# Casts of the folded w2 on GpSimd, later outputs, later reuse of slots, and a sync queue in emission order, in a fused attention and SwiGLU kernel

## The chip, the cores and the metric

The kernel runs on one core of one Trainium2 chip. The metric is the time of one execution on the device in microseconds (us). The engines are named as in the profile: PE is TensorE's matmuls, PEld its weight loads, DVE is VectorE, ACT is ScalarE, POOL is GpSimd, and SP is SyncE, whose queue issues nearly all of the transfers (DMAs).

## What is computed

The input x has 2048 tokens of 512 elements in fp32. Cut to what matters, the reference is:

```python
xn  = layernorm(x)
qkv = (xn @ wqkv)                      # 32 heads of 16
a   = softmax(mask(q @ k.T / sqrt(16))) @ v   # sliding window of 256 tokens
A   = a @ wo
B   = (silu(xn @ w1) * (xn @ w3)) @ w2   # 512 -> 1792 -> 512
out = x + A * silu(B)                  # the kernel's last step
```

The last line is written as the kernel joins the two halves: one output block takes the product with wo, the silu of the feed-forward result and x.

## The kernel before, in words

**Work.** Every matmul of the projections and of the feed-forward part is done on operands that are split in two fp16 pieces, a high and a low one, in three products (high by high, high by low, low by high). The tokens are taken in four tiles t of 512. A tile's attention is 8 units (32 units in all), each a group of heads over the sliding window. A tile's feed-forward part is 14 blocks f of 128 hidden columns: `gate_up` (matmuls at L991, tanh on ACT at L1006, two products on DVE at L1010 and L1015) and then the product with w2, called down. In t=0 down is `down` at L1184, with w2 split as it comes. In t=1 to 3 it is a fast matrix product with seven products in place of eight: activations are folded on POOL and ACT (`fold_first`, L1042 to L1054, and `fold_second`, to L1084, with casts at L1072, subtractions at L1073 and sums at L1078 to L1081), and the 14 blocks are taken in two groups k, of 8 and of 6. A group's seven pieces are `fold_down_piece` (L1114); `unfold` (L1148) puts the seven results together.

**Weights.** In t=0 w1, w3 (L836) and w2 (L877) are loaded raw and split on ACT and POOL (helper lines L329 to L334); the split w1 and w3 are stored to DRAM as dW1 (L997), the split wqkv as dWQ (L589). From t=1 on they come back from there (dW1 at L832, dWQ at L617). The folded w2 is made once, in `fold_weights` (L934 to L976), for seven pairs j of blocks, about when tile 1 begins: raw w2 is loaded (L943) and scaled on ACT (L949), the sums z and y are made on POOL (L951 to L954), and `cut` makes of each of e, o (the scaled rows themselves), z and y a high piece with a cast on ACT (L959) and a low piece with subtractions on POOL (L961). Four steps later the result is stored to dW2 (L966). `load_fold` (L1095) fetches from dW2 the weights of each piece, two pieces ahead of the piece that uses them: 84 loads in three tiles.

**Attention's small transfers.** A unit's maxima go out and come back through DRAM (dm at L691, back into qa at L693). Queries and keys are fetched at L626. The finished results go os to on (L780, four transfers) and their denominators os to dd (L781), dd to dr (L795), after a reciprocal on DVE (L799, L800) dr to de (L802), de to rb (L806, eight transfers); then POOL multiplies by rb (L807 through the helper L329) and casts (L813).

**Output.** `total` (L1209 to L1241) makes one block of 128 tokens: tanh on ACT (L1222), the product with wo on PE (L1228), a product on DVE (L1232), the addition of x on POOL (through L329; on DVE in the last tile), and the store (L1237). Its x comes by `residual` (L1207).

**What sets the order.** Feed-forward pieces are put between the pieces of attention by `spread` and `batches`. A counter of steps, `step`, runs what `later(n, f)` put off by n steps. Working tiles come from a pool of 55 slots: `take` hands out the slot that has been free longest, and `give(tile, after=n)` returns a slot with a date n steps on, so that it is handed out later. `ORDERED` (L54) names the engines whose instructions are issued in the order in which the program emits them. In the kernel before that is PE alone: the queues of ACT, DVE, POOL and SP are put in an order of its own by a scheduler, and `tc.issue_after` holds an instruction behind another one in that order. An engine's queue, once compiled, is strictly in order: an instruction that waits holds all that stand behind it.

Of the kernel before, what the change touches and what calls it, by code (L numbers as in the profile page):

```python
# [17 lines left out]
ENGINE = mybir.EngineType  # L18
# [3 lines left out]
P = 128  # L22
S = 2048
D = 512
# [22 lines left out]
KR = TERMS * DH  # L47
# [3 lines left out]
VW = DH + 1  # L51
VB = 10
SLOTS = 55
ORDERED = {ENGINE.PE}  # L54
GROUPS = ((0, 4), (4, 8), (8, 11), (11, 14))
FOLDS = ((0, 4), (4, 7))
FOLD_AT = (0, 1, 2, 4, 6, 8, 10)
# [25 lines left out]
def tile_block(ctx: ExitStack, tc: tile.TileContext, x, wqkv, wo, w1, w3, w2, out):  # L83
# [142 lines left out]
    dW1 = dram.tile([FB, 2, P, 2 * NC * P], F16, name="dW1")  # L226
    dW2 = dram.tile([7, P, FB // 2, D], F16, name="dW2")


    def squares(parts, on_act=0, apart=0):  # L230

# [335 lines left out]
    def project(t, g, k, terms=(range(3),), scores_bank=False):  # L567


        cell = {}  # L570

        parts = ([[(c, i) for c in (2 * half, 2 * half + 1) for i in range(3)] for half in range(2)] if len(terms) == 1
                 else [[(c, i) for i in group for c in range(NC)] for group in terms])

        def part(n):
            assert turned[t] == 4
            w = WQ[t, g, k]
            xh, xl = X[t]
            if n == 0:
                cell["pp"] = pss.tile([P, 2, TW], F32, name="s")[:, 0, :] if scores_bank else bank([P, TW])  # L580
            for c, i in parts[n]:
                a, b = ((0, xh), (1, xh), (0, xl))[i]
                nc.tensor.matmul(cell["pp"], w[:, (a * NC + c) * P:(a * NC + c + 1) * P], b[:, c, :], start=(c, i) == parts[0][0],  # L583
                                 stop=(c, i) == parts[-1][-1])
            if n < len(parts) - 1:
                return
            if t == 0:
                def store():
                    nc.sync.dma_start(dWQ[g, k], w)  # L589
                    give(w, after=4)  # L590
                later(8, store)
            else:
                give(w)
            pp = cell["pp"]
            both = take(F16)
            B = both.rearrange("p (a t) -> p a t", a=2)
            s = QS / (XS * WS)
            with urgent():
                nc.scalar.activation(B[:, 0, :], pp, AF.Copy, scale=s)

            def rest():
                with urgent():
                    lasts["emptied"] = nc.vector.scalar_tensor_tensor(B[:, 1, :], pp, s, B[:, 0, :], op0=ALU.mult, op1=ALU.subtract)  # L603
                d = (dQ, dK)[k][g][:, :, t * TW:(t + 1) * TW]
                if k == 0:
                    nc.sync.dma_start(d[:, 0:2, :], B[:, 0:1, :].to_broadcast([P, 2, TW]))
                    nc.sync.dma_start(d[:, 2, :], B[:, 1, :])
                else:
                    nc.sync.dma_start(d[:, 0:2, :], B)
                    nc.sync.dma_start(d[:, 2, :], B[:, 0, :])  # L610
                give(both, after=4)
            later(1, rest)
        return opening([(len(l), lambda n=n: part(n)) for n, l in enumerate(parts)])
# [5 lines left out]
    def fetch(t, g):  # L619
        QA[t, g] = qa = qpool.tile([P, 4, TW], F16, name="qa")  # L620
        ka = keys(t, g)
        c0 = 0 if t else 2 * P
        for dst, d in ((ka[:, :, c0:], dK[g][:, :, t * TW - 2 * P + c0:(t + 1) * TW]),
                       (qa, dQ[g][:, :, t * TW:(t + 1) * TW])):
            for r in range(2):
                nc.sync.dma_start(dst[64 * r:64 * r + KR],  # L626
                                  d[64 * r:64 * r + 64].rearrange("(a d) i t -> (d i) a t", d=DH))


# [197 lines left out]
    def load(t, f):  # L827
        if t:
            a = [take(F16) for _ in range(2)]
            WF[t, f] = [a, None]  # L830
            for k in range(2):
                nc.sync.dma_start(a[k], dW1[f, k])  # L832
            return
        RAW[f] = raw = [take(F32) for _ in range(2)]
        for k, w in enumerate((w1, w3)):
            nc.sync.dma_start(raw[k].rearrange("p (c f) -> p c f", f=P),  # L836
                              w[:, f * P:(f + 1) * P].rearrange("(c p) f -> p c f", p=P))

    measured = set()
# [34 lines left out]

    def load_down(f):
        RAW2[f] = raw = take(F32)
        nc.sync.dma_start(raw, w2[f * P:(f + 1) * P, :])  # L877

    def measure_down(k, f):

# [53 lines left out]
    def fold_weights(j):  # L934

        cell = {}
        l, r = slice(0, 256), slice(256, 512)
        sub = nc.gpsimd.tensor_sub

        def load():  # L940
            cell["raw"] = [take(F32) for _ in range(2)]
            for i, raw in enumerate(cell["raw"]):
                nc.sync.dma_start(raw, w2[(2 * j + i) * P:(2 * j + i + 1) * P, :])  # L943

        def sums():
            assert folded
            e, o = cell["raw"]
            for i, raw in enumerate((e, o)):
                nc.scalar.activation(raw, raw, AF.Copy, scale=fold_w[:, 2 * j + i:2 * j + i + 1])  # L949
            cell["z"] = z, y = [take(F32) for _ in range(2)]  # L950
            sub(z[:, l], e[:, r], e[:, l])  # L951
            sub(z[:, r], o[:, r], z[:, l])
            sub(y[:, l], o[:, r], e[:, r])
            sub(y[:, r], o[:, l], z[:, r])  # L954

        def cut(raw, n, which):

            a = take(F16)
            nc.scalar.copy(a[:, 0:n], raw[:, 0:n])  # L959
            for c in range(0, n, 256):  # L960
                sub(a[:, n + c:n + c + 256], raw[:, c:c + 256], a[:, c:c + 256])  # L961
            give(raw, after=6)

            def store():
                for c, i in enumerate(which):
                    nc.sync.dma_start(dW2[i, :, j, :].rearrange("p (h d) -> p h d", h=2),  # L966
                                      a[:, 0:2 * n].rearrange("p (h c d) -> p c h d", h=2, d=256)[:, c])
                give(a, after=4)
            later(4, store)

        def cuts():
            e, o = cell["raw"]
            z, y = cell["z"]
            for n, work in enumerate(((e, 256, (0,)), (o, 512, (1, 2)), (z, 512, (4, 5)), (y, 512, (6, 3)))):
                later(2 * n, lambda work=work: cut(*work))
        return load, sums, cuts  # L976
# [3 lines left out]
    def gate_up(t, f):  # L980
        cell = {}

        def part(k, half):
# [10 lines left out]
                return  # L994
            if t == 0:
                def store():
                    nc.sync.dma_start(dW1[f, k], w)  # L997
                    give(w, after=4)
                later(8, store)
            else:  # L1000
                give(w)
            if k == 0:
                cell["s"] = sg = take(F32)

                with urgent():
                    nc.scalar.activation(sg, cell[0], AF.Tanh, scale=sg_scale[:, f:f + 1])  # L1006

                def product():
                    with urgent():
                        lasts["emptied"] = nc.vector.scalar_tensor_tensor(sg, sg, 1.0, cell[0], op0=ALU.add, op1=ALU.mult)  # L1010
                later(1, product)
            else:
                sg = cell["s"]
                with urgent():
                    lasts["emptied"] = nc.vector.scalar_tensor_tensor(sg, cell[1], 0.5 * HS / (WS * XS)**2, sg,  # L1015
                                                                      op0=ALU.mult, op1=ALU.mult)
                if t:
                    HH[t, f] = sg
                    later(1, lambda: (fold_second if f % 2 else fold_first)(t, f // 2))
                    return  # L1020
                HH[t, f] = hh = take(F16)

                def rest():
                    nc.scalar.copy(hh[:, 0:TW], sg)  # L1024
                    halves(nc.gpsimd.tensor_sub, hh[:, TW:], sg, hh[:, 0:TW])
                    give(sg, after=4)
                later(1, rest)
        return [q for k in range(2) for q in opening([(6, lambda k=k, half=half: part(k, half)) for half in range(2)])]

# [27 lines left out]
    def fold_second(t, j):  # L1057
# [7 lines left out]
        def cut(raw, view, which, give_too=()):  # L1065
# [7 lines left out]
                sub(lo[:, k], view[:, k], hi[:, k])  # L1073
            for k, i in enumerate(which):
                operand(t, j, i, made, 512, 256 * k)
            give(raw, *give_too, after=4)

        nc.gpsimd.tensor_add(z[:, 0], ee[:, 1], oo[:, 1])  # L1078
        sub(z[:, 1], z[:, 0], ee[:, 0])
# [8 lines left out]
    def load_fold(t, k, i):  # L1088
# [3 lines left out]
        for j in range(j0, j1, 2):  # L1092
            made.append(take(F16))
            n = min(2, j1 - j)
            nc.sync.dma_start(made[-1].rearrange("p (j d) -> p j d", d=D)[:, 0:n], dW2[i, :, j:j + n, :])  # L1095

    QS7 = {}

# [39 lines left out]
    def unfold(t):  # L1138
# [14 lines left out]
        into(0, 0, q[0], q[1])  # L1153
        halves(add, q[5], q[5], q[4])
        into(0, 1, q[5], q[2])
        give(*q, after=6)
        summed.update((t, b) for b in range(4))

    def folds(t, k):
# [353 lines left out]
    for n in range(len(units)):  # L1513
# [6 lines left out]
                    ahead[n].append((0, lambda k=k, half=half: load_qk(*tiles[k], half)))  # L1520
        if n % 8 >= 4 and t < NT - 1:
            beside[n] += value(4 * t + n % 8)
        if 2 <= n % 8 < 6 and t:
            beside[n] += [(0, lambda t=t, b=n % 8 - 2: residual(t - 1, b))] + total(t - 1, n % 8 - 2)
        beside[n] += ahead[n]
    other = [sum(c for c, _ in b) for b in beside]
    a_unit = (whole - KEEP - EARLY + sum(other)) / len(units)
# [55 lines left out]
```

## Time and profile before

| | |
|---|---|
| time of the kernel before | 861.5 us, median of 3 runs (861.15 to 862.03) |
| time of the profiled execution | 859.68 us |
| its span, first to last instruction | 857.9 us |
| mean granted clock of PE | 0.982 |
| PE busy | 804.5 us of the span |
| DVE, POOL, ACT busy | 635.0, 416.1, 402.1 us |
| bytes moved by DMA | 133.82 MB, mean 156 GB/s |

A row of a group of instructions reads: line, engine, operation, output and input tiles, shape, number; then the busy time in us and the mean of one in ns; then how long the engine had been idle ahead of them and what ended most of that. A row of a timeline reads: start, duration, engine and line, and in brackets the idle time ahead of it with its releaser. For SP ("SPq") the duration is the issue of the transfers, not their landing. The window view gives the busy time of each engine in a stretch, and PEclk, the granted clock.

### The profile page before, as it was taken

The page shows a single profiled execution, that of the slowest core. Times are in us where ns is not written, and L with a number is a line of the kernel's source. Part 1 is how long each engine was busy: PE and PEld are TensorE (multiplying, and loading weights), DVE is VectorE, ACT ScalarE, POOL GpSimd, SP SyncE. Part 2 cuts the span into 40 slices and gives each one's busy share as a digit, 9 for nine tenths or more (in the row PEclk, how much of TensorE's full clock was granted, in tenths as well). Part 3 has the DMA queues.
Part 4 walks back from the last instruction along what each step waited for, and adds up shares of the span by engine and source line. Part 5 has one row for each costly group of instructions (what it writes and reads, how often), then busy time and mean ns, then how long its engine had stood idle before and what let it go on. Part 6 is the DMA issues. An engine that isn't in the chain of part 4 may idle for free.

```text
span 857.9 us, 24287 instructions
## 1 busy us (share of the span) xinstructions
PE 804.5 (94%) x9302; PEld 420.7 (49%) x9302; DVE 635.0 (74%) x2027; ACT 402.1 (47%) x597; POOL 416.1 (49%) x723
## 2 busy tenths in 40 slices
PE   8998988999999499998999898999999989999997
PEld 4444444444444245654447454456544644457464
DVE  8886796788886378675888777875688778774447
ACT  6899774544565244453443233443444334334411
POOL 2248064341768936346362746421146458551561
PEclk9999999999999799999999999999999999999999
DMA  9999654248356483757554444554545545324411
GB/s 283 259 286 293 197 156 124 90 131 238 90 166 177 113 232 111 231 173 218 163 155 122 152 115 137 144 157 125 160 121 144 138 141 152 109 83 129 127 34 62
DMA packets 118421, 133.82 MB, mean 156 GB/s; under 512 B 19168, under 2 KB 76832, under 8 KB 118304
## 3 DMA queue, kind: packets, MB, share of 16 engines
q1 hardware_dynamic: 118016, 131.74, 52.4%
q8 instruction: 73, 1.20, 0.6%
q10 hardware_dynamic: 288, 0.52, 0.2%
q14 instruction: 44, 0.36, 0.2%
HBM read 94.50 MB, written 33.42 MB: 149 GB/s over the span
## 4 chain that ended last, share of the span: by engine, by line
PE 56%; DVE 14%; POOL 11%; DMA 6%; ACT 5%; issue 4%; SPq 2%; POOLq 0%; ACTq 0%; DVEq 0%
PE m L991 21%; PE m L1114 10%; PE po L758 6%; PE m L583 5%; DVE junk L664 4%; PE m L1228 4%; PE s L730 4%; DMA slot<-in_B_w_dram 3%; POOL slot L329 3%; PE m L553 2%; POOL slot L1073 2%; PE s L650 2%; PE m L1184 2%; DVE s L737 2%; ACT pt L740 1%
## 5 line engine op out<-in xcount | busy, mean ns | idle before, releaser
L991 PE MATMUL m<-XH,slot 128*128 128x512 f16 x896 | 272.9, 387 | 7.5 <-DVE slot L603 4.5
L740 ACT ACTIVATE pt<-s,es 128x1024 f32<-128x1024 f32 x152 | 167.6, 1113 | 157.8 <-DVE s L737 154.7
L991 PEld LDWEIGHTS <-slot 128*128 128x128 f16 x1344 | 126.2, 99 | 166.8 <-issue 28.3
L329 POOL TENSOR_TENSOR slot<-slot,slot 128x256 f16<-128x256 f32 (+1 forms) x156 | 104.2, 697 | 146.0 <-ACT slot L1024 68.2
L991 PE MATMUL m<-XL,slot 128*128 128x512 f16 x448 | 172.5, 385 | 0.0
L737 DVE TENSOR_TENSOR s<-s,MK 128x256 f32<-128x256 f32 (+2 forms) x280 | 119.2, 435 | 57.6 <-PE s L730 54.4
L664 DVE CUSTOM_DVE_ANT_0 junk<-s,MW 128x320 bf16<-128x320 f32 x276 | 134.1, 486 | 20.5 <-PE s L650 11.6
L1114 PE MATMUL m<-slot,slot 128*128 128x256 f16 x882 | 102.7, 273 | 1.9 <-POOL slot L1073 1.2
L1114 PEld LDWEIGHTS <-slot 128*128 128x128 f16 x882 | 84.4, 98 | 19.1 <-issue 5.1
L664 DVE CUSTOM_DVE_ANT_0 junk<-po,MW 128x320 bf16<-128x320 f32 x172 | 83.6, 486 | 5.7 <-DVE al L288 0.5
L583 PE MATMUL m<-XH,slot 128*128 128x512 f16 x240 | 72.4, 386 | 12.8 <-DVE slot L1010 12.8
L1073 POOL TENSOR_TENSOR slot<-slot,slot 128x256 f16<-128x256 f32 x126 | 82.7, 676 | 0.6
L758 PE MATMUL po<-pt,V 64*32 64x320 f32 (+4 forms) x2880 | 77.2, 342 | 0.0
L1010 DVE SCALAR_TENSOR_TENSOR slot<-slot,m 128x512 f32<-128x512 f32 x56 | 38.3, 684 | 43.7 <-ACT slot L1006 43.6
L730 PE MATMUL s<-qa,KA 50*64 50x320 f16 (+3 forms) x1472 | 59.2, 261 | 7.2 <-ACT pt L740 5.0
L583 PEld LDWEIGHTS <-slot 128*128 128x128 f16 x384 | 36.1, 99 | 56.7 <-issue 17.4
L758 PEld LDWEIGHTS po<-pt,V 64*32 64x32 f32 x2880 | 50.3, 106 | 22.3 <-issue 0.8
L730 PEld LDWEIGHTS <-KA 50*64 50x64 f16 x1472 | 31.0, 106 | 58.4 <-issue 38.9
L1078 POOL TENSOR_TENSOR slot<-slot,slot 128x256 f32<-128x256 f32 x21 | 15.3, 728 | 89.4 <-DVE slot L1015 89.4
L1006 ACT ACTIVATE slot<-m,sgs 128x512 f32<-128x512 f32 x56 | 38.2, 682 | 37.9 <-PE m L991 37.8
L329 POOL TENSOR_TENSOR on<-on,rb 128x256 f32<-128x256 f32 x32 | 23.4, 752 | 57.4 <-DMA rb<-de 57.3
L650 PE MATMUL s<-KA,qa 48*64 48x320 f16 (+3 forms) x824 | 45.4, 296 | 4.0 <-ACT pt L740 2.4
(186 smaller groups left out, 1170.7 us busy)
## 6 DMA issues: line engine op xcount, KB each, us to landing
slot<-dW SPq DMA_DIRECT2D x147, 256.0 KB
slot<-in_B_w_dram SPq DMA_DIRECT2D x56, 256.0 KB
slot<-in_A_x_dram SPq DMA_DIRECT2D x30, 256.0 KB
dW<-slot SPq DMA_DIRECT2D x28, 256.0 KB
KA<-dK SPq DMA_DIRECT2D x24, 288.0 KB
dW<-slot SPq DMA_DIRECT2D x49, 128.0 KB
qa<-dQ SPq DMA_DIRECT2D x32, 192.0 KB
slot<-dWQ SPq DMA_DIRECT2D x24, 256.0 KB
```

What stands on the lines that cost most here:

```text
L329: op(out[:, c], a[:, c], b[:, c])
L583: nc.tensor.matmul(cell["pp"], w[:, (a * NC + c) * P:(a * NC + c + 1) * P], b[:, c, :], start=(c, i) == parts[0][0], stop=(c, i) == parts[ ...
L650: nc.tensor.matmul(s[c:c + w, r, :n], qa[rows, 2 * p + a, ii * P + c:ii * P + c + w], ka[rows, 2 * p + a, e - n:e], start=True, stop=True)
L664: lasts["maximum"] = nc.vector.tensor_tensor_reduce(out=junk[:, :n], in0=s[:, r, :n], in1=mask, scale=1.0, scalar=NEG, op0=ALU.add, op1=AL ...
L730: nc.tensor.matmul(s[64 * h:64 * h + 64, r, o:o + 64 * n], ka[rows, 2 * p + a, 64 * (m + 4):64 * (m + 5)], qa[rows, 2 * p + a, 64 * (m + k ...
L737: nc.vector.tensor_add(v, v, MK[:, kind, of:of + n, :].unsqueeze(1).to_broadcast([P, 2 * len(which), n, 64]))
L740: nc.scalar.activation(pt, s, AF.Exp, scale=es)
L758: nc.tensor.matmul(cell["po"][32 * i:32 * i + 32, h, 64 * (m + k):64 * (m + k + n)], V[64 * h:64 * h + 64, (4 * t + m // 2) % VB, hd * VW: ...
L991: nc.tensor.matmul(cell[k], w[:, (a * NC + c) * P:(a * NC + c + 1) * P], b[:, c, :], start=c == 0 and i == 0, stop=c == NC - 1 and i == 2)
L1010: lasts["emptied"] = nc.vector.scalar_tensor_tensor(sg, sg, 1.0, cell[0], op0=ALU.add, op1=ALU.mult)
L1073: sub(lo[:, k], view[:, k], hi[:, k])
L1114: nc.tensor.matmul(ps, made[:, f:f + P], wj[:, 256 * b:256 * b + 256], start=j == j0 and n == 0, stop=j == j1 - 1 and n == 2)
```

## The change

- SP joins the engines that issue in emission order. The sync queue takes every transfer where the program emits it.
- `behind_load` holds stores to dWQ (L589, the one shown), dW1 (L997) and dW2 (L966) behind the latest load that the program has recorded in `lasts["load"]` (at L626, shown, and in the same way at L832, L836, L877 and L1095).
- In `fold_weights`, `cut` makes the casts of z and y on GpSimd, each in two halves of 256 columns: 28 casts of 128x256 on POOL in place of 14 of 128x512 on ACT. Those of e and o stay on ACT.
- Slots are returned with later dates: raw of `cut` 14 in place of 6, raw of `fold_second` 14 in place of 4, sg in t=0 8 in place of 4, q of `unfold` 16 in place of 6.
- `total` and `residual` of the tile before come one unit later in the units of t=2 and t=3; in t=1 they stay where they were. The last tile's own are unchanged.

The compiled programs hold the same 944 transfers on SP and the same matmuls.

```diff
-ORDERED = {ENGINE.PE}
+ORDERED = {ENGINE.PE, ENGINE.SP}
...
+    def behind_load():
+        return tc.issue_after(lasts["load"].ins) if "load" in lasts else nullcontext()
...
-                    nc.sync.dma_start(dWQ[g, k], w)
+                    with behind_load():
+                        nc.sync.dma_start(dWQ[g, k], w)
...
-                nc.sync.dma_start(dst[64 * r:64 * r + KR],
+                lasts["load"] = nc.sync.dma_start(dst[64 * r:64 * r + KR],
...
         def cut(raw, n, which):
             a = take(F16)
-            nc.scalar.copy(a[:, 0:n], raw[:, 0:n])
+            if any(raw is r for r in cell["raw"]):
+                nc.scalar.copy(a[:, 0:n], raw[:, 0:n])
             for c in range(0, n, 256):
+                if not any(raw is r for r in cell["raw"]):
+                    nc.gpsimd.tensor_copy(a[:, c:c + 256], raw[:, c:c + 256])
                 sub(a[:, n + c:n + c + 256], raw[:, c:c + 256], a[:, c:c + 256])
-            give(raw, after=6)
+            give(raw, after=14)
...
-                    give(sg, after=4)
+                    give(sg, after=8)
...
-            give(raw, *give_too, after=4)
+            give(raw, *give_too, after=14)
...
-        give(*q, after=6)
+        give(*q, after=16)
...
-        if 2 <= n % 8 < 6 and t:
-            beside[n] += [(0, lambda t=t, b=n % 8 - 2: residual(t - 1, b))] + total(t - 1, n % 8 - 2)
+        b = n % 8 - (2 if t == 1 else 3)
+        if 0 <= b < 4 and t:
+            beside[n] += [(0, lambda t=t, b=b: residual(t - 1, b))] + total(t - 1, b)
```

More of the change, by code (lines that the diff above doesn't have):

```diff
@@ L831, in load @@
             for k in range(2):
-                nc.sync.dma_start(a[k], dW1[f, k])
+                lasts["load"] = nc.sync.dma_start(a[k], dW1[f, k])
             return
@@ L835, in load @@
         for k, w in enumerate((w1, w3)):
-            nc.sync.dma_start(raw[k].rearrange("p (c f) -> p c f", f=P),
+            lasts["load"] = nc.sync.dma_start(raw[k].rearrange("p (c f) -> p c f", f=P),
                               w[:, f * P:(f + 1) * P].rearrange("(c p) f -> p c f", p=P))
@@ L876, in load_down @@
         RAW2[f] = raw = take(F32)
-        nc.sync.dma_start(raw, w2[f * P:(f + 1) * P, :])
+        lasts["load"] = nc.sync.dma_start(raw, w2[f * P:(f + 1) * P, :])
     def measure_down(k, f):
@@ L958, in cut @@
             a = take(F16)
-            nc.scalar.copy(a[:, 0:n], raw[:, 0:n])
+            if any(raw is r for r in cell["raw"]):
+                nc.scalar.copy(a[:, 0:n], raw[:, 0:n])
             for c in range(0, n, 256):
+                if not any(raw is r for r in cell["raw"]):
+                    nc.gpsimd.tensor_copy(a[:, c:c + 256], raw[:, c:c + 256])
                 sub(a[:, n + c:n + c + 256], raw[:, c:c + 256], a[:, c:c + 256])
-            give(raw, after=6)
+            give(raw, after=14)
             def store():
                 for c, i in enumerate(which):
-                    nc.sync.dma_start(dW2[i, :, j, :].rearrange("p (h d) -> p h d", h=2),
-                                      a[:, 0:2 * n].rearrange("p (h c d) -> p c h d", h=2, d=256)[:, c])
+                    with behind_load():
+                        nc.sync.dma_start(dW2[i, :, j, :].rearrange("p (h d) -> p h d", h=2),
+                                          a[:, 0:2 * n].rearrange("p (h c d) -> p c h d", h=2, d=256)[:, c])
                 give(a, after=4)
@@ L996, in store @@
                 def store():
-                    nc.sync.dma_start(dW1[f, k], w)
+                    with behind_load():
+                        nc.sync.dma_start(dW1[f, k], w)
                     give(w, after=4)
@@ L1094, in load_fold @@
             n = min(2, j1 - j)
-            nc.sync.dma_start(made[-1].rearrange("p (j d) -> p j d", d=D)[:, 0:n], dW2[i, :, j:j + n, :])
+            lasts["load"] = nc.sync.dma_start(made[-1].rearrange("p (j d) -> p j d", d=D)[:, 0:n], dW2[i, :, j:j + n, :])
     QS7 = {}
```

## The prediction

> **What bounds the kernel now.** I read the page first, then PE's waits by stretch, then the timelines of ACT and PE around the longest wait, then SP's queue.
>
> ```profile
> span 857.9 us, 24287 instructions
> PE 804.5 (94%) x9302; PEld 420.7 (49%) x9302; DVE 635.0 (74%) x2027; ACT 402.1 (47%) x597; POOL 416.1 (49%) x723
> PEclk9999999999999799999999999999999999999999
> L991 PE MATMUL m<-XH,slot 128*128 128x512 f16 x896 | 272.9, 387 | 7.5 <-DVE slot L603 4.5
> ```
>
> PE is busy for 804.5 of 857.9 us, so at most 53.4 us can be won without touching its work, and the change touches none of it. A gain must come out of PE's pauses. The one slice with a granted clock below 0.9 is the 14th, 279 to 300 us. The waits of PE from 150 to 300 us, and the timelines of ACT and of PE there, show why:
>
> ```profile
> PE m L583 <- DVE slot L1010: 12.2, 2, 11.0
> ```
>
> ```profile
> 287.74 1.45 ACT L959 CAST slot<-slot 128x256 f16<-128x256 f32 x3 [9.01 <-POOL slot L1073]
> ...
> 294.67 0.68 ACT L1006 ACTIVATE slot<-m,sgs 128x512 f32<-128x512 f32 x1
> ```
>
> ```profile
> 296.12 1.01 PE L583 MATMUL m<-XH,slot 128*128 128x512 f16 x2 [11.03 <-DVE slot L1010]
> 296.93 0.63 PE L583 MATMUL m<-XL,slot 128*128 128x512 f16 x1
> ...
> 300.92 0.38 PE L583 MATMUL m<-XL,slot 128*128 128x512 f16 x1
> ```
>
> This is the **knot**. ACT stands for 9.01 us before a cast of `fold_weights`, whose slot POOL (L1073) still holds. The tanh (L1006) is behind it in ACT's queue, DVE's product behind the tanh, PE behind DVE, which stands for 11.03 us. Then PE runs at half clock: 0.63 us for a matmul that takes 0.38 later. From 296.1 to 299.7 us, 3.6 us x (1 - 0.38/0.63) = 1.4 us. The knot costs 12.4 us in all.
>
> **Why POOL is late there.** Windows of 250 to 317, 284 to 300 and 395 to 403 us, and the groups of POOL and of ACT from 205 to 345 us (ACT's with shapes apart):
>
> ```profile
> 250.00:317.00 67.00, 53.75 (x675) 25.43 (x668) 40.24 (x122) 31.81 (x49) 51.71 (x85) 0.90 0.58 170
> 284.00:300.00 16.00, 4.97 (x31) 1.92 (x29) 2.67 (x8) 6.21 (x11) 15.94 (x28) 0.68 0.44 119
> 395.00:403.00 8.00, 5.66 (x43) 2.31 (x42) 3.33 (x11) 5.15 (x7) 5.08 (x8) 0.79 0.48 148
> ```
>
> ```profile
> L961 POOL TENSOR_TENSOR slot<-slot,slot 128x256 f16<-128x256 f32 x35 | 22.7, 677 | 11.5 <-ACT slot L959 11.5
> L1072 POOL CAST slot<-slot 128x256 f16<-128x256 f32 x16 | 6.2, 399 | 4.7 <-issue 4.5
> ```
>
> ```profile
> L959 ACT CAST slot<-slot 128x512 f16<-128x512 f32 x15 | 9.0, 615 | 12.4 <-POOL slot L1073 5.4 <-POOL slot L952 3.1 <-DMA dK<-slot 1.6
> ```
>
> POOL is the fullest engine of that stage after PE (15.94 of 16 us inside the knot), and it stood still for 11.5 us because it waited for ACT's casts: each engine held the other.
>
> **The change part by part.**
>
> *Casts of z and y.* 28 casts of 128x256 on POOL at 0.399 us (L1072, the same shape) add 11.2 us to POOL; 14 casts at 0.615 us take 8.6 us off ACT. POOL's low pieces no longer wait for ACT, and the cast that held the tanh is e's or o's alone. With that and the later reuse of raw (14 steps), the wait of 9.01 us goes: **-12.4 us** with its clock.
>
> What is late next: I laid POOL's queue of the changed program, in its compiled order, out with the durations of these groups from 250.4 us on. It is 113 instructions and 70.6 us without a gap, up to the subtraction L961 that ends at 321. A tanh of the first output block (L1222) waits for that subtraction's slot, and stands in ACT's compiled order ahead of an exp:
>
> ```profile
> 320.18 0.62 ACT L1222 ACTIVATE slot<-slot 128x512 f32<-128x512 f32 x1
> 322.80 1.11 ACT L740 ACTIVATE pt<-s,es 128x1024 f32<-128x1024 f32 x1 [2.00 <-DVE s L737]
> ```
>
> If the knot is gone, that exp is due at 322.8 - 12.4 = 310.4, and the tanh lets it start at about 321.6: 11.2 us late. From both sides: 0, if POOL's work does not delay it; 11.2, if all of it does. I take **+9**, near the upper end, as POOL's queue has no gap in which to catch up; with a half-clock window, **+1.4**. So the knot mostly moves.
>
> *The sync queue in emission order.* In before, SP's order differs: loads stand far ahead. Of `load_fold`'s 84 loads the first and the last issue at 300.0 and 811.1 us; the pieces that use them run later. The instructions of L1095 and then those of L1114 in four windows (336 to 376, 452 to 478, 667 to 692, 765 to 795):
>
> ```profile
> L1095 SPq DMA_DIRECT2D slot<-dW x84: 319/376/1336, 300.0 to 811.1; - x84
> ```
>
> ```profile
> L1114 PE MATMUL m<-slot,slot x168: 272/273/283, 338.1 to 373.9; 128*128 128x256 f16 x168
> ```
>
> ```profile
> L1114 PE MATMUL m<-slot,slot x126: 269/273/283, 453.0 to 475.8; 128*128 128x256 f16 x126
> ```
>
> ```profile
> L1114 PE MATMUL m<-slot,slot x126: 272/273/283, 667.8 to 689.8; 128*128 128x256 f16 x126
> ```
>
> ```profile
> L1114 PE MATMUL m<-slot,slot x168: 272/273/283, 766.5 to 792.8; 128*128 128x256 f16 x168
> ```
>
> In the changed program a load stands where it is emitted, two pieces ahead of its use (2 x 35.8/7 = 10 us in the first of these groups, 2 x 22.8/7 = 6.5 in the second), behind every transfer emitted before it. Those wait for engines, one in line. SP in before, 324 to 374 us and its waits:
>
> ```profile
> 336.55 0.36 SPq L1237 DMA_DIRECT2D out_dram<-slot  x1
> ...
> 350.63 0.38 SPq L691 DMA_DIRECT2D dm<-mt  x1
> ...
> 354.79 0.55 SPq L693 DMA_DIRECT2D qa<-dm  x2
> ...
> 371.79 2.24 SPq L806 DMA_DIRECT2D rb<-de  x5
> ```
>
> ```profile
> SPq L780 <- DVE os L774: 33.8, 10, 7.2
> SPq L693 <- DMA dm<-mt: 21.1, 16, 3.3
> ...
> SPq L1237 <- POOL slot L329: 16.3, 7, 5.9
> ```
>
> An issue costs 2.24/5 = 0.45 us; a transfer through DRAM and back holds the queue for 354.79 - 350.63 = 4.2 us at most. For the landing of a 256 KB load I take 3.4 us (an estimate between nothing and that 4.2, near the upper end since it moves more).
>
> First group of t=1: the output store issues when POOL's addition is done, 336.55, and in emission order 37 transfers stand from it to a load of a piece. 37 x 0.45 = 16.6, and waits of 2.7 (rb for de), 0.8 (L780) and 3.8 (qa for dm) that those transfers meet: issue at 336.6 + 23.9 = 360.5, landed at 363.9. The piece runs at 354.1 in before: 9.8 us late. Bounds 0 and 9.8: the store's own addition moves earlier if the knot shrinks, and one late load gives the rest time. I take the middle, **+5**.
>
> The other groups by the same walk. Second of t=1: L1095 issues at 459.0 and 470.5, lands at 462.4 and 473.9, needed at 460.9 and 469.5: up to 4.4, I take **+3.5**. Second of t=2: issue 679.6, landed 683.0, needed 678.5: 4.5, **+4**. First of t=3, behind the moved output stores: issue 789.0, landed 792.4, needed 788.4: 4.0, **+3**. The first of t=2 has slack.
>
> Second of t=3, the last thing ahead of the end; SP and PE there:
>
> ```profile
> 810.13 1.33 SPq L1095 DMA_DIRECT2D slot<-dW  x3
> ...
> 824.53 2.44 SPq L780 DMA_DIRECT2D on<-os  x4
> 827.02 0.53 SPq L781 DMA_DIRECT2D dd<-os  x1
> 828.72 0.33 SPq L795 DMA_DIRECT2D dr<-dd  x1
> ```
>
> ```profile
> 826.50 3.00 PE L1114 MATMUL m<-slot,slot 128*128 128x256 f16 x26
> 830.72 11.09 PE L1114 MATMUL m<-slot,slot 128*128 128x256 f16 x100 [1.21 <-POOL slot L1073]
> ```
>
> The first loads of this group are emitted directly ahead of it, behind L780, L781, L795 and two loads of x: issue at 828.7 + 0.3 + 2 x 0.45 = 829.9, landed at 833.3, needed at 827.2. 6.1 late, of which 1.2 is spent now in waiting for POOL: 4.9, I take **+4.5**. Each of these groups lies between 0 (the queue is ahead after all) and the figure of the walk.
>
> *Clock.* A pause of 2.34 us brings a half-clock window as well:
>
> ```profile
> 398.10 0.42 PE L730 MATMUL s<-qa,KA 50*64 50x320 f16 x11 [2.34 <-ACT pt L740]
> ```
>
> The window 395 to 403 has 0.79: 8 x 0.21/0.5 = 3.4 us at half clock, 1.4 us lost. Of the five new stalls I charge one in full, **+1.4** (0 to 7). [...]
>
> *The rest at nothing.* In t=0 the raw loads (L836, L877) also lose their lead; the walk leaves them 0 to 13 us of slack, so 0, with -2 to +2. `behind_load` does nothing once SP is in emission order: the last load is already ahead. Later dates only change which slot is taken. Later outputs: the same matmuls, one unit on, PE has the work either way; their stores are priced in the walk.
>
> **Sum.** -12.4 + 9 + 1.4 + 5 + 3.5 + 4 + 3 + 4.5 + 1.4 = +19.4 us. Against the profiled execution 859.7 + 19.4 = 879.1. The median is 1.8 above that execution: 880.9. I predict **881 us**.
>
> **Rivals.**
> *The knot goes and does not form again; loads late:* 861.5 - 12.4 + 21.4 - 4 (the output store comes earlier) = 866.5, say 867. For it: the tanh (L1222) may be given its place where POOL is through. Against: POOL has 70.6 us of work without a gap.
> *The other side, faster:* the queue keeps up, since two pieces give it 6.5 to 10 us; the knot is gone without return. It decides at one point: whether the loads of the pieces issue less than 6.5 - 3.4 = 3.1 us after they are emitted. Then 861.5 - 12.4 + 2 = 851. For it: nothing in before waits long on loads. Against: SP's waits of 33.8, 21.1 and 16.3 us are in line now.
> *Delay feeds on itself:* full 11.2, 9.8 and the walk's figures of the groups (4.4, 4.5, 4.0, 4.9), 7 of clock: 861.5 - 12.4 + 1.4 + 45.8 = 896.
> *It does not do what it says:* the casts change nothing, as the wait is for L1073 and not for z or y, and the queue is hidden: 861.5.
>
> **How the numbers follow.** Forecast 0.57 (its own range 871 to 891), knot gone with late loads 0.18, faster 0.13, worse 0.07, as before 0.05. The range from 862 to 898 leaves out the faster case, the unchanged one and a tail: 0.2. A measurement of this kernel tells 0.2% (1.7 us) from no change. Faster by more: 0.14; within: 0.04; slower: 0.82.
>
> **What would show it.** In the changed profile PE should wait at L1114 for DMAs into slots (dW), several us in t=1 and t=3, where it now waits for none; the wait of 11.0 us at L583 should be gone from 285, and one of like size stand near 310 to 325, behind an exp (L740) or a tanh with ACT waiting for L961. POOL should hold 28 more casts and ACT 14 fewer. If PE shows no wait on those loads, the walk of the queue is wrong; if ACT has no wait of over 4 us on POOL from 300 to 330, the second knot is.

## The result and the profile after

The changed kernel takes 958.5 us (median of 3 runs, 955.3 to 959.35) against 861.5: 1.113 times as long, with an interval of 1.111 to 1.116. The direction was forecast, the size was not: +97 us where +19 were forecast, outside the range.

The lines of the changed file have moved. L583 is now L587, L617 is L622, L650 is L655, L664 is L669, L689 is L694, L691 is L696, L693 is L698, L730 is L735, L740 is L745, L774 is L779, L780 is L785, L802 is L807, L806 is L811, L832 is L837, L959 is L965, L961 is L969, L966 is L975, L991 is L1000, L1006 is L1016, L1010 is L1020, L1073 is L1083, L1095 is L1105, L1114 is L1124, L1222 is L1232, L1237 is L1247, and the helper L329 is L333. First the page of the profile after:

```profile
span 953.5 us, 24246 instructions
PE 824.9 (87%) x9302; PEld 426.1 (45%) x9302; DVE 636.1 (67%) x2027; ACT 395.7 (41%) x583; POOL 426.4 (45%) x751
PEclk9999998998999697999798899989999999999989
L587 PE MATMUL m<-XH,slot 128*128 128x512 f16 x240 | 80.5, 424 | 63.2 <-DMA slot<-dWQ 54.2
```

The span grew by 95.6 us, and two terms make it up. PE is busy 20.4 us longer with the same 9302 matmuls, because more of them ran at half clock (PE is busy for 67.2 us at a granted clock of 0.50 where before had 23.9; the row of the granted clock has six 8s, two 7s and a 6 where before had one 7; the mean is 0.945 against 0.982). The other 75.2 us are pauses: PE stands still for 128.6 us of the span instead of 53.4, with nineteen pauses of over 2 us instead of five. PE's waits in the changed kernel say for what:

```profile
PE m L587 <- DMA slot<-dWQ: 54.2, 8, 13.9
PE m L1124 <- DMA slot<-dW: 18.9, 7, 6.3
PE m L1000 <- DMA slot<-dW: 14.7, 3, 8.0
PE s L735 <- DMA qa<-dm: 11.3, 1, 11.3
PE m L587 <- DVE slot L1020: 8.5, 4, 5.5
```

Read each as: what waited and for what, us in total, times, the longest. Four DMAs hold PE for 99.1 us. In before no DMA held it for more than 0.5. The largest, the loads of the projection weights from dWQ, has no term in the prediction at all. The loads of the folded w2 (L1124), on which the prediction spent its sum, cost 18.9.

Set matmul by matmul against before, in the times of before, the changed kernel is 0.8 us ahead at 220, 8.6 ahead at 310, 13.9 behind at 330, 73 behind at 480 and 95.6 behind at the end. Tile 1 loses most: its stretch has the stores of the folded w2, the backlog of GpSimd and the output stores in one queue.

Two places show the mechanism. The first, in SP's timeline:

```profile
286.93 0.38 SPq L975 DMA_DIRECT2D dW<-slot  x1
302.25 2.45 SPq L785 DMA_DIRECT2D on<-os  x4
...
313.71 0.33 SPq L696 DMA_DIRECT2D dm<-mt  x1
317.66 0.55 SPq L698 DMA_DIRECT2D qa<-dm  x2
```

The queue stands from 287.3 to 302.2 before on<-os. GpSimd's timeline there ends with

```profile
301.54 0.68 POOL L333 TENSOR_TENSOR slot<-on,slot 128x256 f16<-128x256 f32 x1
```

the last read of the tile on by the earlier unit. There is one buffer of on, so the transfer into it must wait for GpSimd's backlog. The maxima were ready long before, as DVE's timeline shows, and are emitted behind on<-os:

```profile
292.73 0.27 DVE L694 CAST mt<-s 32x128 f16<-32x128 f32 x1
```

Their store goes out 20.7 us after 293.0: 9.2 us of that are the rest of the hold, the other 11.5 the sixteen transfers that stand between, with their own waits. PE waits for it:

```profile
319.13 0.85 PE L735 MATMUL s<-qa,KA 50*64 50x256 f16 x8 [11.30 <-DMA qa<-dm]
```

The second place is 50 us later, SP again:

```profile
351.32 0.34 SPq L1247 DMA_DIRECT2D out_dram<-slot  x1
351.70 1.27 SPq L807 DMA_DIRECT2D de<-dr  x1
354.30 3.56 SPq L811 DMA_DIRECT2D rb<-de  x8
...
362.92 2.44 SPq L785 DMA_DIRECT2D on<-os  x4
...
365.98 0.44 SPq L622 DMA_DIRECT2D slot<-dWQ  x1
```

An output store waits for GpSimd's addition, which ends at 351.3; the transfers of the denominators for a round trip through DRAM, 2.6 us from de<-dr to rb<-de; on<-os for GpSimd's use of rb and on, which ends at 362.9; and a weight load that waits for nothing stands last. PE needed it at 354.8:

```profile
368.70 1.03 PE L587 MATMUL m<-XH,slot 128*128 128x512 f16 x2 [13.94 <-DMA slot<-dWQ]
369.52 0.63 PE L587 MATMUL m<-XL,slot 128*128 128x512 f16 x1
```

In before the load for this place was issued at 321.88, for a matmul at 340.70, as these rows of SP and PE of the kernel before show:

```profile
321.88 0.32 SPq L617 DMA_DIRECT2D slot<-dWQ  x1
```

```profile
340.70 0.59 PE L583 MATMUL m<-XH,slot 128*128 128x512 f16 x2
```

The program emits it only 3.1 us ahead of that matmul (at the PE instruction of 337.6 us, by the order of emission in the compiled program). The scheduler had let it issue 15.7 us ahead of that place. Over all 24 such loads, before issues them 7 to 54 us ahead of the place where the program emits them, and eight of them are emitted 3.1 us or less ahead of their use. In the changed kernel they issue between 3 us before and 23 us behind that place. Seven of the eight waits for dWQ, 50.5 of the 54.2 us, stand at loads of these eight.

### The profile page after: what moved, and what is told of

The parts are those of the page before. It is cut to its first block, busy times and chain, and to the rows that moved or that the text cites. A ratio compares the mean times of both kernels' runs of the same rounds, so it can differ in the third digit from the quotient of the medians.

```text
span 953.5 us, 24246 instructions
## 1 busy us (share of the span) xinstructions
PE 824.9 (87%) x9302; PEld 426.1 (45%) x9302; DVE 636.1 (67%) x2027; ACT 395.7 (41%) x583; POOL 426.4 (45%) x751
## 4 chain that ended last, share of the span: by engine, by line
PE 50%; DMA 15%; DVE 10%; POOL 9%; SPq 9%; issue 4%; ACT 3%; DVEq 0%; POOLq 0%; ACTq 0%
PE m L1000 16%; PE m L1124 8%; PE m L587 7%; PE po L763 5%; DMA slot<-dW 3%; PE s L735 3%; DVE junk L669 3%; PE m L1238 3%; PE m L1194 3%; PE m L557 3%; SPq L785 3%; DMA slot<-dWQ 2%; DMA dm<-mt 2%; POOL slot L333 2%; SPq L811 2%
## 5 line engine op out<-in xcount | busy, mean ns | idle before, releaser
L1000 PE MATMUL m<-XH,slot 128*128 128x512 f16 x896 | 272.1, 386 | 17.3 <-DMA slot<-dW 14.7
L745 ACT ACTIVATE pt<-s,es 128x1024 f32<-128x1024 f32 x152 | 167.4, 1113 | 219.2 <-DVE s L742 214.7
L1000 PEld LDWEIGHTS <-slot 128*128 128x128 f16 x1344 | 125.8, 99 | 175.9 <-issue 21.8
L333 POOL TENSOR_TENSOR slot<-slot,slot 128x256 f16<-128x256 f32 (+1 forms) x156 | 103.7, 695 | 182.8 <-ACT slot L1034 68.3
L1000 PE MATMUL m<-XL,slot 128*128 128x512 f16 x448 | 171.9, 384 | 0.0
L669 DVE CUSTOM_DVE_ANT_0 junk<-s,MW 128x320 bf16<-128x320 f32 x276 | 134.1, 486 | 27.0 <-PE s L655 17.7
L587 PE MATMUL m<-XH,slot 128*128 128x512 f16 x240 | 80.5, 424 | 63.2 <-DMA slot<-dWQ 54.2
L1124 PE MATMUL m<-slot,slot 128*128 128x256 f16 x882 | 111.3, 286 | 18.9 <-DMA slot<-dW 18.9
L1124 PEld LDWEIGHTS <-slot 128*128 128x128 f16 x882 | 87.7, 102 | 41.4 <-DMA slot<-dW 21.4
L587 PEld LDWEIGHTS <-slot 128*128 128x128 f16 x384 | 37.4, 105 | 116.7 <-DMA slot<-dWQ 58.4
L669 DVE CUSTOM_DVE_ANT_0 junk<-po,MW 128x320 bf16<-128x320 f32 x172 | 83.6, 486 | 5.3 <-DVE al L292 0.4
L1083 POOL TENSOR_TENSOR slot<-slot,slot 128x256 f16<-128x256 f32 x126 | 82.0, 672 | 0.6
L1016 ACT ACTIVATE slot<-m,sgs 128x512 f32<-128x512 f32 x56 | 38.3, 683 | 101.2 <-PE m L1000 72.5
L735 PE MATMUL s<-qa,KA 50*64 50x320 f16 (+3 forms) x1472 | 60.9, 267 | 12.7 <-DMA qa<-dm 11.3
L1020 DVE SCALAR_TENSOR_TENSOR slot<-slot,m 128x512 f32<-128x512 f32 x56 | 38.3, 684 | 50.1 <-ACT slot L1016 48.4
L735 PEld LDWEIGHTS <-KA 50*64 50x64 f16 x1472 | 31.2, 108 | 66.2 <-issue 48.2
L1082 POOL CAST slot<-slot 128x256 f16<-128x256 f32 x84 | 33.1, 408 | 39.4 <-PE m L1124 24.0
L655 PE MATMUL s<-KA,qa 48*64 48x320 f16 (+3 forms) x824 | 47.0, 301 | 3.5 <-ACT pt L745 3.2
```

The costliest lines, as they stand in the source:

```text
L333: op(out[:, c], a[:, c], b[:, c])
L655: nc.tensor.matmul(s[c:c + w, r, :n], qa[rows, 2 * p + a, ii * P + c:ii * P + c + w], ka[rows, 2 * p + a, e - n:e], start=True, stop=True)
L669: lasts["maximum"] = nc.vector.tensor_tensor_reduce(out=junk[:, :n], in0=s[:, r, :n], in1=mask, scale=1.0, scalar=NEG, op0=ALU.add, op1=AL ...
L735: nc.tensor.matmul(s[64 * h:64 * h + 64, r, o:o + 64 * n], ka[rows, 2 * p + a, 64 * (m + 4):64 * (m + 5)], qa[rows, 2 * p + a, 64 * (m + k ...
L745: nc.scalar.activation(pt, s, AF.Exp, scale=es)
L1000: nc.tensor.matmul(cell[k], w[:, (a * NC + c) * P:(a * NC + c + 1) * P], b[:, c, :], start=c == 0 and i == 0, stop=c == NC - 1 and i == 2)
```

## The experiments

Two theories were set against each other. **H, holds:** a transfer that waits in the ordered queue holds the loads behind it. **L, leads:** the loads are emitted too late, whether anything holds them or not. A third, **T**, was that the moves themselves (casts on GpSimd, later outputs) cost the time. A single run is given as such; the kernel before ran on the same chip each time, at 858.6 to 861.0 us.

**1. The moves without the order.**

```diff
-ORDERED = {ENGINE.PE, ENGINE.SP}
+ORDERED = {ENGINE.PE}
```

> The changed kernel with the sync queue put back under the scheduler: casts on GpSimd, later outputs and later reuse stay. Theory H (transfers that wait in the sync queue hold the weight loads behind them): PE's waits on DMA vanish and the knot at 285 is gone, 848 to 866 us. Rival T (the moves themselves load GpSimd with 11.2 us and the outputs come too late, the queue's order matters little): 930 us or more.

860.6 us, 1.0003 times before (0.998 to 1.002). T is out: the moves alone cost nothing on balance. They bring nothing either, and the profile shows where the 12.4 us of the knot went. PE's waits, then ACT's timeline:

```profile
PE s L655 <- ACT pt L745: 11.8, 4, 9.6
PE s L655 <- DVE M L669: 7.1, 1, 7.1
```

```profile
302.86 0.41 ACT L965 CAST slot<-slot 128x256 f16<-128x256 f32 x1 [13.27 <-DMA dW<-slot]
...
325.07 0.63 ACT L1232 ACTIVATE slot<-slot 128x512 f32<-128x512 f32 x1 [5.76 <-POOL slot L969]
```

The pause at 285 is gone. Two others stand at 294.7 (9.6 us; a cast on ACT waits 13.3 us for a slot whose store to dW2 has not landed) and at 319.9 (7.1 us; the tanh of the first output block waits for a subtraction on GpSimd, and DVE's product behind the tanh stands ahead of what PE needs).

**2. The order without the moves.** The reverse edit on the kernel before.

> The kernel before with only the sync queue in emission order. Theory H: most of the loss is here, 900 to 950 us, with PE waiting tens of us for dWQ and dW loads. Rival T: 870 us or less. If it is about 925, GpSimd's casts add some 30 us by holding the queue longer.

973.9 us, 1.130 times before (1.127 to 1.134). PE's waits:

```profile
PE m L583 <- DMA slot<-dWQ: 66.5, 10, 13.5
PE m L1114 <- DMA slot<-dW: 27.9, 8, 7.1
PE m L991 <- DMA slot<-dW: 14.1, 3, 7.7
```

The order alone makes the whole loss, +114 us, more than the 900 to 950 us of theory H. With the moves the time is 15 us shorter, so nothing shows that the casts add to it.

**3. Two buffers of on** (and 54 slots, for the room), on the changed kernel.

```diff
-ON[t, g] = (opool.tile([P, TW], F32, name="on", bufs=1), ...
+ON[t, g] = (opool.tile([P, TW], F32, name="on", bufs=2), ...
```

> The changed kernel with two buffers for the tile on in place of one (and 54 slots in place of 55, for the room). The transfers on<-os then no longer wait for GpSimd's last subtraction on the earlier unit. Theory H: the hold of 15 us at 287 to 302 us and the 11.3 us wait for qa<-dm go, 915 to 945 us. Rival L (loads are simply emitted too late, no hold is needed for that): within 5 us of 958.

927.6 us, one run: 31 us back. SP no longer stands at 287 us, and PE's wait of 11.3 us for the maxima is gone. What is left:

```profile
PE m L587 <- DMA slot<-dWQ: 44.3, 8, 12.7
PE m L1124 <- DMA slot<-dW: 19.9, 6, 7.1
```

The hold by the one buffer is a part of the cause. It leaves four fifths of the waiting for dWQ.

**4. Later output stores**, 8 steps later for the first three tiles.

```diff
-                nc.sync.dma_start(out[r, :], y)
-                give(y, XR[t, b], after=6)
+                def store():
+                    nc.sync.dma_start(out[r, :], y)
+                    give(y, XR[t, b], after=6)
+                if t < NT - 1:
+                    later(8, store)
+                else:
+                    store()
```

> The changed kernel with the output stores of the first three tiles emitted 8 steps later, when GpSimd's addition is done. The sync queue's 40.3 us of waiting for that addition goes. Theory H: 925 to 950 us. Rival L: within 5 us of 958.

957.1 us, one run: nothing. SP's 40.3 us of waiting for GpSimd's additions vanished from its waits, and the next transfers in line took the time over (SP in this run, then in the changed kernel):

```profile
SPq L785 <- DVE os L779: 146.0, 23, 13.0
...
SPq L785 <- POOL slot L333: 45.4, 12, 16.1
```

```profile
SPq L785 <- DVE os L779: 114.2, 22, 11.5
...
SPq L785 <- POOL slot L333: 37.7, 12, 14.1
```

The waits of the queue are no prices. Taking one away is worth nothing if the next transfer would have waited as long.

**5. dWQ loads one unit earlier.**

```diff
-                if u == n + 1 and tiles[k][0]:
+                if u == n + 2 and tiles[k][0]:
                     ahead[n].append((0, lambda k=k, half=half: load_qk(*tiles[k], half)))
```

> The changed kernel with the loads of the projection weights from dWQ emitted one unit (about 25 us) earlier. Theory L (leads too short): PE's 54.2 us of waiting for dWQ and most of the half clock behind it go, 885 to 905 us. Theory H (holds in the queue): the loads come in time as well, but the held queue makes other transfers late in their place, 905 to 940 us.

918.7 us, one run: 40 us back, with no wait for dWQ left among PE's large ones. The time lies in the range of H, and a part of the waiting passed to others, as H said:

```profile
PE m L1124 <- DMA slot<-dW: 37.0, 11, 9.9
PE m L1000 <- DMA slot<-dW: 19.1, 3, 12.7
```

**6. Later on<-os.** The transfers on<-os and dd<-os, and what follows from them, 4 steps later (`later(4, send)` around them); no load is moved.

> The changed kernel with the transfers on<-os and dd<-os emitted 4 steps later (about 12 us), and what follows from them as much later; the loads stay where they were. Theory H: the queue no longer stands before the loads of dWQ, whose waits fall under 25 us: 905 to 935 us. Theory L: the loads have leads as short as before, 945 us or more.

914.4 us, one run: 44 us back. The wait for dWQ falls to 28.6 us with the leads as they were. So H and L both act: about half of the waiting for dWQ (25.6 of 54.2 us) came from the transfers emitted ahead of the loads. H had expected a little less to be left, under 25 us.

**7. Later return of the maxima**, qa<-dm one step after dm<-mt (`later(1, back)`).

> The changed kernel with the return of the maxima (qa<-dm) emitted one step after their store. The 95.5 us that the queue waits for dm to land shrink. Theory H: 930 to 952 us. Theory L: within 5 us of 958, or slower where PE waits for qa.

955.9 us, one run. It tells nothing of H: the queue still waits 90.6 us for dm to land (95.5 before the edit), so one step was not enough to take the hold away.

**8. dWQ one unit earlier and the folded w2 four pieces ahead.**

```diff
-            if n + 2 < 7:
-                pieces.append(loads[n + 2])
+            if n + 4 < 7:
+                pieces.append(loads[n + 4])
...
-        return loads[:2], pieces
+        return loads[:4], pieces
```

> The changed kernel with dWQ loads one unit earlier and the loads of the folded w2 four pieces ahead in place of two. Theory L: both DMA waits of PE go (54.2 and 18.9 us with their half clock), 865 to 885 us. Theory H: 900 us or more, as the held queue passes its delay to dW1, the maxima and the queries.

891.4 us, one run, 67 us back; between the two expectations.

**9. All leads and later on<-os; 10. all leads and two buffers of on; 11. all leads alone.** To run 8 these add: the last group of the fold loads two blocks earlier, and the first dW1 loads of tiles 2 and 3 ahead of the fold that precedes them.

> The changed kernel with everything that helped put together: dWQ loads a unit earlier, folded w2 four pieces ahead (the last group two blocks earlier), the first dW1 loads of the tiles 2 and 3 ahead of the fold that precedes them, and on<-os, dd<-os 4 steps later. If holds and short leads together are the whole cause, this comes back to 855 to 870 us. If the order costs something else, it stays above 880.

> The same leads as in the run beside it, but with two buffers of on (54 slots) in place of the later on<-os. If the hold by GpSimd's use of on is what is left after the leads, 860 to 875 us; if the wait for os itself holds the queue as much, 5 to 15 us slower than the run beside it.

> All the longer leads of the loads on the changed kernel, with one buffer of on (55 slots). Against the run with the same leads and two buffers (865.6): the difference is the hold by GpSimd's use of on when the leads are mended. Expected 875 to 890 us, if hold and leads add; 865 us, if long leads make the hold harmless.

880.4 us (1.023 times before, 1.021 to 1.026) with later on<-os; **865.6 us**, one run, with two buffers; 883.5 us, one run, with the leads alone. Two buffers are worth 31 us without the leads and 18 with them; the leads 75 us with one buffer and 62 with two. Together they return 93 of the 97 us. (These differences are between single runs, on chips on which the kernel before differs by up to 2.4 us.) Later on<-os did not do so, against what was expected of it: pauses of 2 to 4.4 us on changing engines are left in that run, and PE stays busy for 815.3 us. Which of its delays makes that stays open. The page of the run with two buffers, and its waits:

```profile
PE 802.9 (93%) x9302; PEld 419.7 (49%) x9302; DVE 633.4 (73%) x2027; ACT 395.3 (46%) x583; POOL 427.9 (50%) x751
```

```profile
PE m L1000 <- DVE slot L1020: 11.1, 1, 11.1
PE m L1000 <- DMA slot<-dW: 10.2, 3, 5.1
PE s L735 <- DMA qa<-dm: 6.3, 1, 6.3
```

Most of the half clock has gone with the pauses (802.9 us busy, a mean clock of 0.978). One pause of 11.1 us behind ACT is left, up to 313.3 us, of the size of the first knot. ACT stands there before the tanh of the first output block, for a slot that GpSimd still holds:

```profile
311.27 0.63 ACT L1232 ACTIVATE slot<-slot 128x512 f32<-128x512 f32 x1 [13.77 <-POOL slot L1083]
```

**12. That kernel with the casts of z and y back on ACT.**

> The kernel with the longer leads and two buffers of on, with the casts of z and y back on ACT. It had one wait of 11.1 us at 302 us behind ACT. If the casts on GpSimd make that wait, 850 to 858 us, faster than both kernels; if it forms by slots anyway, 862 to 870 us.

864.9 us (1.006, 1.004 to 1.009). The wait of 11.1 us is not there, and several of 3 to 6 us are, so that its going gains nothing. No version beat the kernel before.

**13. Two buffers of on in the kernel before.**

> A control: the kernel before with two buffers of on and 54 slots, its sync queue under the scheduler. If two buffers help only against the hold in an ordered queue, 858 to 864 us; if they are worth something by themselves, 850 to 857 us.

864.3 us (1.004, 1.002 to 1.007). The two buffers (with one slot less) gain nothing where the scheduler orders SP's queue; what they gain in the others belongs to the order.

**14. Later dates alone and 15. casts on GpSimd alone**, on the kernel before.

> The kernel before with the later dates of the slots alone; casts, outputs and the sync queue as before. If the knot at 285 us is only the choice of slot (ACT's cast gets a slot that GpSimd still holds), it goes: 848 to 856 us. If GpSimd's lateness itself is the cause, it forms again at another slot: 858 to 864 us.

> The kernel before with the casts of z and y on GpSimd alone. 11.2 us more on GpSimd, 8.6 less on ACT. If the knot comes from ACT and GpSimd holding each other, 850 to 858 us; if from GpSimd being full, 862 to 872 us.

866.3 us (1.006, 1.004 to 1.008) and 864.7 us (1.004, 1.003 to 1.006). ACT in the first and in the second:

```profile
292.97 0.92 ACT L959 CAST slot<-slot 128x512 f16<-128x512 f32 x2 [7.54 <-POOL slot L1073]
```

```profile
287.85 0.40 ACT L960 CAST slot<-slot 128x256 f16<-128x256 f32 x1 [8.91 <-POOL slot L1076]
```

With the dates alone the cast waits again, 7.5 us; with the casts alone 8.9, in the same place. Neither edit removes the knot alone. Each costs 4 to 5 us by itself (the dates come out above both of their expectations), while all moves together (run 1) cost nothing; whether the later outputs or the combination makes up for it was not separated.

## Why the prediction was wrong, point by point

**The step that failed** is "the sync queue in emission order": of the loads after tile 0 it priced those of the folded w2 and no others. dWQ (54.2 us of waiting), dW1 (14.7) and the return of the maxima (11.3) stood nowhere in the sum as waits of PE, not even at nothing. The prediction's own rule, that a load's lead is the distance from where it is emitted to where it is used, gives 3.1 us or less for eight dWQ loads, less than the 3.4 us that it took for a landing (in the changed kernel PE went on 2.7 to 5.1 us after the late ones were issued). Its own walk even passes one of them: of the 37 transfers behind the output store of 336.55 the 18th is a dWQ load. By the figures of the walk it issues at 336.6 + 18 x 0.45 + 2.7 + 0.8 = 348.2, has landed at 351.6 and is needed at 340.7: 10.9 us late, where 13.9 was measured. Run 5 shows that these short leads cost (40 us back), run 6 that the transfers ahead of the loads do (44 us back).

**The holds were mis-read.** The walk let each transfer wait as long as it did in before. In before on<-os waits for GpSimd's last read of on as well, in a row of SP's waits that the prediction passes over:

```profile
SPq L780 <- POOL slot L329: 15.5, 6, 4.6
```

In the ordered queue this wait grew to 37.7 us in twelve, the longest 14.1 (the hold at 287), and run 3 shows it to be a cause. That the delay feeds back (a late weight makes PE late, PE makes os late, os holds the queue) is likely, but not shown: SP still waits 94.3 us for os in run 10, at 865.6 us, against 114.2 in the changed kernel. The rival "delay feeds on itself" named this at 0.07 and priced it at 896.

**The folded w2** was priced at +5 +3.5 +4 +3 +4.5 = 20, and PE waited 18.9 us. The groups came out at 0 in the first of tile 1 (PE stood before dWQ there instead), 6.2 in the second, 0 and 3.4 in tile 2, 3.0 and 6.3 in tile 3. The mechanism was right, but that the sum came so near was luck: one group priced at 5 came to nothing, and the second groups of tiles 1 and 3 lie above their own bounds of 4.4 and 4.9.

**The clock** was charged with two stretches at half clock, 2.8 us, with bounds of 0 to 7 for the new stalls; it took 20.4. The trace has sixteen such stretches in place of seven, 105.8 us in all in place of 30.7 (PE stood still anyway in 38.7 and 6.9 us of them). What the term had too small is the number of pauses and the length of the stretches at the long ones (13.7 us at each of the three pauses of over 11 us, where the term took 3.4).

**The knot.** It goes, as forecast, and it forms again, as forecast (+9 and a stretch at half clock). Run 1 shows it apart from the order, with 9.6 us at 294.7 and 7.1 at 319.9, the second through the very tanh and subtraction that the prediction named. The first came through a slot whose store was late, which it did not name. In the changed kernel itself the same backlog of GpSimd reaches PE through SP's queue, as 11.3 us of waiting for the maxima at 307.8. ACT stands there too, but for a slot whose store to DRAM is late, and not for GpSimd:

```profile
320.77 0.69 ACT L1016 ACTIVATE slot<-m,sgs 128x512 f32<-128x512 f32 x1 [17.65 <-DMA dW<-slot]
```

So by the prediction's own sign, "if ACT has no wait of over 4 us on POOL from 300 to 330", its second knot is wrong for the changed kernel. A wait of the size that it gave, 11.1 us behind the same tanh, stands in run 10 alone, and there ACT waits for another of GpSimd's subtractions (L1083 and not L969).

**At nothing.** Tile 0 was right at its end (0.8 us ahead at 220), as a balance: the changed kernel is 6.4 us ahead at 150 and loses most of it in a pause of 5.5. Later outputs were not separated from the rest of the moves; all moves together are worth 0 without the order, and 15 us under it, for a reason that stays open.

**The rivals.** "Faster" needed loads of the pieces that issue less than 3.1 us after they are emitted; 57 of the 84 issued later than that, up to 15.5 us after it. The range ended at 898, because every bound in it belonged to a transfer that the walk had counted.

## What to carry to other kernels

When a queue loses its scheduler, list every transfer that it carries, and for each the distance between where the program emits it and where it is used. What the scheduler had moved forward is what can come late (here dWQ, up to 23 us behind its place), and a load that needs nothing is as late as the slowest transfer ahead of it (here it issued at 365.98 us, behind on<-os at 362.92). Repair the leads of the loads first, then the single buffers that hold the queue; the sum of the queue's waits does not tell which of them costs (in run 4 40.3 us of them went, and 1.4 us of the time).

## What the runs showed of the hardware that was not expected

A pause of PE does not bring half clock by its length alone. The window view at two pauses of the changed kernel, one of 2.31 us that ended at 289.3 and one of 2.17 us that ended at 762.4 (the number after POOL's is the granted clock):

```profile
287.00:297.00 10.00, 7.69 (x64) 3.47 (x63) 8.35 (x24) 5.60 (x8) 9.92 (x19) 1.00 0.30 100
...
760.00:768.00 8.00, 4.59 (x27) 2.98 (x25) 2.80 (x9) 1.11 (x1) 3.20 (x5) 0.79 0.66 185
```

The longer of the two cost no clock (1.00), the shorter 3.4 us at half rate (0.79 over 8 us). Of the 24 pauses of over 2 us in before and after, the 14 of 3.7 us or more all brought half clock; of the ten of 2.0 to 3.4 us seven did, and three, of 2.31, 3.02 and 3.31 us, did not. What tells the three from the seven stays open.

Within the two spans all stretches at half clock last 3.4, 6.8, 10.2 or 13.7 us, and the starts in before lie whole multiples of 3.41 us apart (142.67 and 265.55 us: 36 of them).

At the pause of 13.9 us the stretch lasted 13.7 us, from 359.9 to 373.6, and PE stood still for the first 8.8 of it; the matmuls after the pause took 627 ns in place of 386:

```profile
L587 PE MATMUL m<-XH,slot 128*128 128x512 f16 x4 | 2.1, 627 | 13.9 <-DMA slot<-dWQ 13.9
```
